# Low parts of split weights moved from GpSimd to VectorE, and a second set of weight load buffers

## The chip, the cores and the metric

The kernel runs on one core of one Trainium2 chip. The metric is the device time of one execution in microseconds. Engines are named as in the profile: PE is TensorE's matmul, PEld its weight load, DVE is VectorE, ACT is ScalarE, POOL is GpSimd, SP is SyncE, whose queue issues nearly all loads.

## The reference

Three blocks follow each other, all in float32:

```python
scores = scale * q @ k.T + bias            # 2 x 8 heads, 768 positions, 64 wide, local band + 8 global keys
x = softmax(scores) @ v                    # -> x: 1536 tokens x 512
xn = x / rms(x) * rms_g
x = (silu(xn @ w_gate) * (xn @ w_val)) @ w_out     # 512 -> 1536 -> 512, float64 weights
e = argmax(x @ r_gate)                     # 8 experts, one per token
out[e == i] = gate * (relu(x[e == i] @ w1[i]) @ w2[i])   # 512 -> 1024 -> 512
```

## The kernel before, in words

To keep float32 accuracy, each large product is made of three matmuls on float32r operands: every operand is split into a high part (its rounding to float32r) and a low part (the rest), and high x high, low x high and high x low are summed in PSUM. ACT makes the high part by a copy that rounds. The low part is a subtraction, value minus high part. Activations are split between ACT and DVE or POOL, weights between ACT and POOL, or ACT, DVE and POOL together.

The program has four parts, all written out in one stream for the usual inputs (`body(True)`):

- The attention, up to about 175 us, with the first part of the gated layer mixed into it.
- The gated layer in three sweeps over the 1536 features: sweep 0 takes blocks 0 to 2 of 128 features, sweep 1 blocks 3 to 6, sweep 2 blocks 7 to 11. Each sweep goes over six stages of 256 tokens (`moe_block`) and adds into the twelve row tiles `part0` to `part11` of 128 tokens. A stage and block needs 24 matmuls into two PSUM banks (L766), then tanh on ACT (L774), two products on DVE (`th` L775, `hf` L779), high part on ACT (L783), low part on POOL (L784), and then the output product (L803).
- The weights of this layer arrive as float64 and are turned into float32 while the sweep before runs: `convert64` takes a raw block of 512 KB, and for each half does one ACT operation (L333), four on DVE (L336, L339, L342, L345), the high part on ACT (L352) and the low part on POOL (L353). This is done 36 times. 9 belong to blocks 0 to 2 and are done during the attention; 27 to blocks 3 to 11 and are done behind it.
- The experts. In sweep 2 the tokens are routed (`route`), stored to the DRAM tensor `x1d` (L814), and their slots written to small tables. Expert by expert the token rows are gathered by POOL (L969), turned by PE (L982), multiplied by `w1` (L1055 for tiles of 128 tokens, L1029 for pairs of 256), and by `w2` (L1007), scaled on ACT (L1013) and scattered by POOL (L1014). Expert 0 has two tiles of 128 tokens, which take their own path (`expert_tile`: relu `hr` L1062, turned by PE L1069, split by L1073 and L1074); experts 1 to 7 go as pairs (`expert_pair`: high part `eh` L1037 on ACT, low part L1038 on DVE).

The weights of an expert come in eight chunks of 128 x 1024 (`prep_chunk`): SP loads a chunk into one of three raw buffers (L945, `NRAW = 3`), ACT makes the high part of all 1024 columns (L947), DVE the low part of the first 512 (L950, `NDV = 512`) and POOL that of the last 512 (L953). The raw buffer is free when all three are done. The finished chunk lies in a ring of 13 tiles (`ew`), where it stays until PE has used it.

```python
raw = rp.tile([P, DF2], F32, tag="raw", bufs=NRAW, name="rawe")
nc.sync.dma_start(out=..., in_=src)
cp = nc.scalar.activation(out=t[:, 0], in_=raw, func=ACTF.Copy)
nc.vector.tensor_tensor(out=t[:, 1, 0:NDV], in0=raw[:, 0:NDV], ..., op=ALU.subtract)
nc.gpsimd.tensor_tensor(out=t[:, 1, NDV:], in0=raw[:, NDV:], ..., op=ALU.subtract)
```

The order on each engine is set by the framework, which places the instructions by its own estimate of a timeline. Each engine then works through its list strictly in order, so an instruction that waits holds up all that stand behind it. The last loads before the experts, the copies of expert 1's first chunks (pinned behind `eh` of the first tile by `pin["act"]`) and the gathers are placed around the end of sweep 2.

Of the kernel before, what the change touches and what calls it, by code (L numbers as in the profile page):

```python
# [8 lines left out]
F32 = mybir.dt.float32  # L9
# [5 lines left out]
ALU = mybir.AluOpType  # L15
# [4 lines left out]
P = 128  # L20
B, H, S, D = 2, 8, 768, 64
NT, DM, DFF = B * S, H * D, 1536
NE, DF2 = 8, 1024
KD = DM // P
NP = H // 2
TT = NT // P
# [19 lines left out]
def kernel(  # L46
# [16 lines left out]
    nc = tc.nc  # L63
# [11 lines left out]
    NDV = 512  # L75
    HP = 0
    NRAW = 3
# [91 lines left out]
    def behind(i, first):  # L169

        tc.add_manual_dep(
            i.ins, first.ins.name,
            mybir.DependencyInfo(mybir.DependencyClass.NoSync, mybir.DependencyReason.DATA), reason="order",
        )
# [58 lines left out]

    part = [rp.tile([P, DM], F32, name=f"part{i}") for i in range(TT)]
    first_pairs = []
# [53 lines left out]
    def body(is_fast):  # L289
# [37 lines left out]
        def convert64(raw, hi, lo):  # L327
# [23 lines left out]
            else:  # L351
                nc.scalar.activation(out=hi, in_=tf, func=ACTF.Copy)  # L352
            nc.gpsimd.tensor_tensor(out=lo, in0=tf, in1=hi.bitcast(F32), op=ALU.subtract)  # L353

        weights = {}
        pin = {"act": None, "dve": None, "th": None}

# [576 lines left out]

        ring = {"n": 0, "pools": None, "xg": 0}

# [5 lines left out]

        def prep_chunk(src):
            raw = rp.tile([P, DF2], F32, tag="raw", bufs=NRAW, name="rawe")
            nc.sync.dma_start(out=raw if src.ndim == 2 else raw.rearrange("p (a d) -> p a d", a=2), in_=src)  # L945
            t = chunk_tile()
            cp = nc.scalar.activation(out=t[:, 0], in_=raw, func=ACTF.Copy)  # L947
            if pin["act"] is not None:
                behind(cp, pin["act"])
            nc.vector.tensor_tensor(  # L950
                out=t[:, 1, 0:NDV], in0=raw[:, 0:NDV], in1=t[:, 0, 0:NDV].bitcast(F32), op=ALU.subtract
            )
            nc.gpsimd.tensor_tensor(  # L953
                out=t[:, 1, NDV:], in0=raw[:, NDV:], in1=t[:, 0, NDV:].bitcast(F32), op=ALU.subtract
            )
            return t
# [225 lines left out]
        apool_cm.__exit__(None, None, None)  # L1182
        pin["act"] = None
        ea_cm = tc.tile_pool(name="ea", bufs=1, side="right")
# [56 lines left out]
        def prep_next(e, todo, n=1):  # L1241
            for _ in range(n):
                if todo:
                    d, f, c = todo.pop(0)
                    d[e].append(prep_chunk(f(e, c)))

# [117 lines left out]
```

## Time and profile before

| what | value |
|---|---|
| time, median of 3 runs | 671.49 us (669.6, 671.49, 671.59) |
| the profiled execution's own time | 670.62 us |
| its span, first to last instruction | 668.9 us |
| PE busy | 633.8 us, 95% |
| PEld busy | 564.5 us, 84% |
| DVE busy | 439.6 us, 66% |
| ACT busy | 318.3 us, 48% |
| POOL busy | 327.6 us, 49% |
| bytes moved | 83.00 MB, 124 GB/s over the span |

PE is busy for almost the whole span, so the time is that of PE's work plus the short stretches in which PE waits. Shares of the other engines are averages over parts with different loads; they are to be read by stretch. A row of waits says who waited, for which line, how long in total, how often and how long at most. A row of instruction groups gives the line, the engine, what it writes and reads, how often, its busy time and mean duration, and the idle time before it with its releaser.

### The profile page before, as it was taken

The numbers are of one execution on the slowest core, as the hardware profiler recorded it, in microseconds if no ns is written. First come the engines' busy times: TensorE is split into PE (matmuls) and PEld (weight loads), VectorE is DVE, ScalarE is ACT, GpSimd is POOL, SyncE is SP. The second block draws the span as 40 slices with busy tenths as digits, with TensorE's granted clock in tenths as the row PEclk, the third lists the DMA queues.
The fourth block names the chain that finished last, engine by engine and source line by source line (L and its number), as shares of the span: only waits on it lengthen the run. The fifth ranks groups of instructions, "written<-read, shape, count | busy, mean of one in ns | idle before, by whom it ended". The sixth has DMA issues, their size and how long they took to land. (4 is left out here: it accounts for less than half of the span.)

```text
span 668.9 us, 11962 instructions
## 1 busy us (share of the span) xinstructions
PE 633.8 (95%) x4280; PEld 564.5 (84%) x4281; DVE 439.6 (66%) x1203; ACT 318.3 (48%) x620; POOL 327.6 (49%) x358
## 2 busy tenths in 40 slices
PE   9998998999998999999999999899998999999992
PEld 4667888899997899999999999897787898899891
DVE  5765988974699887675369999944366554644410
ACT  3666798775555433334512221333455555564420
POOL 4425758572365544333222433462867758676400
PEclk9999999899999999999999999899999999999997
DMA  7536466541044432212321010321777677667200
GB/s 231 146 112 179 126 190 170 163 117 37 5 151 128 126 96 95 64 64 87 104 64 63 10 57 33 111 84 48 238 228 239 216 237 211 200 201 211 81 13 29
DMA packets 56570, 83.00 MB, mean 124 GB/s; under 512 B 7983, under 2 KB 38703, under 8 KB 56496
## 3 DMA queue, kind: packets, MB, share of 16 engines
q1 hardware_dynamic: 53552, 74.75, 36.8%
q0 software_dynamic: 2944, 7.35, 3.2%
q8 instruction: 37, 0.61, 0.4%
q14 instruction: 37, 0.30, 0.1%
HBM read 75.75 MB, written 7.39 MB: 124 GB/s over the span
## 5 line engine op out<-in xcount | busy, mean ns | idle before, releaser
L766 PE MATMUL pg<-xn,gv 128*128 128x256 f32 x1728 | 229.9, 286 | 2.8 <-DVE th L775 2.2
L766 PEld LDWEIGHTS pg<-xn,gv 128*128 128x128 f32 x1728 | 220.7, 193 | 10.4 <-DVE th L775 2.8
L953 POOL TENSOR_TENSOR ew<-rawe,ew 128x512 fp32r<-128x512 f32 x64 | 98.8, 1558 | 46.3 <-ACT ew L947 45.1
L803 PE MATMUL po<-ow,hid 128*128 128x512 f32 x432 | 113.6, 396 | 2.4 <-DVE th L775 1.1
L784 POOL TENSOR_TENSOR hid<-hf,hid 128x256 fp32r<-128x256 f32 x72 | 59.0, 823 | 108.5 <-ACT hid L783 108.1
L950 DVE TENSOR_TENSOR ew<-rawe,ew 128x512 fp32r<-128x512 f32 x64 | 67.1, 1054 | 63.7 <-ACT ew L947 61.0
L947 ACT ACTIVATE ew<-rawe 128x1024 fp32r<-128x1024 f32 x64 | 67.0, 1063 | 68.8 <-DMA rawe<-in_moe_w_dram 53.2
L1007 PE MATMUL py<-ew,eh 128*128 128x512 f32 x384 | 91.8, 396 | 2.6 <-DVE eh L1038 1.9
L803 PEld LDWEIGHTS po<-ow,hid 128*128 128x128 f32 x432 | 75.7, 189 | 15.3 <-DVE th L775 1.5
L1007 PEld LDWEIGHTS py<-ew,eh 128*128 128x128 f32 x384 | 71.3, 188 | 19.7 <-DVE eh L1038 2.6
L1029 PE MATMUL ph<-xs,ew 128*128 128x256 f32 x672 | 83.7, 284 | 0.4 <-DVE eh L1038 0.4
L1029 PEld LDWEIGHTS ph<-xs,ew 128*128 128x128 f32 x672 | 81.9, 191 | 1.4 <-DVE eh L1038 0.6
L783 ACT ACTIVATE hid<-hf 128x256 fp32r<-128x256 f32 x72 | 29.8, 415 | 87.3 <-DVE hf L779 87.1
L836 DVE CUSTOM_DVE_ANT_0 jk<-part,rgb 128x256 bf16<-128x256 f32 x128 | 59.5, 507 | 0.0
L558 ACT ACTIVATE pr<-pr,mx 128x256 f32<-128x256 f32 (+1 forms) x96 | 45.1, 484 | 15.0 <-DVE mx L554 14.1
L353 POOL TENSOR_TENSOR gv<-cv,gv 128x512 fp32r<-128x512 f32 x24 | 33.1, 1380 | 29.4 <-ACT gv L352 29.1
L775 DVE SCALAR_TENSOR_TENSOR th<-th,pg 128x256 f32<-128x256 f32 x72 | 29.8, 414 | 26.8 <-ACT th L774 26.6
L774 ACT ACTIVATE th<-pg 128x256 f32<-128x256 f32 x72 | 26.9, 376 | 33.3 <-PE pg L766 31.8
L342 DVE SCALAR_TENSOR_TENSOR cv<-raw,cv 128x512 uint32<-128x512 uint32 x36 | 38.0, 1054 | 0.8
L779 DVE SCALAR_TENSOR_TENSOR hf<-th,pg 128x256 f32<-128x256 f32 x72 | 29.7, 414 | 9.3 <-PE pg L766 7.0
L812 DVE TENSOR_TENSOR part<-part,po 128x512 f32<-128x512 f32 x36 | 23.3, 682 | 19.0 <-PE po L803 19.0
L569 PE MATMUL pp<-ident,pr 128*128 128x128 f32 x176 | 32.5, 281 | 2.9 <-ACT ptS L577 2.3
(175 smaller groups left out, 882.1 us busy)
## 6 DMA issues: line engine op xcount, KB each, us to landing
rawe<-in_moe_w_dram SPq DMA_DIRECT2D x64, 512.0 KB, 3.8
raw<-in_moe_w_gate_dram SPq DMA_DIRECT2D x12, 512.0 KB, 3.7
raw<-in_moe_w_val_dram SPq DMA_DIRECT2D x12, 512.0 KB, 3.6
raw<-in_moe_w_out_dram SPq DMA_DIRECT2D x12, 512.0 KB, 3.5
kn<-in_k_dram SPq DMA_DIRECT2D x28, 192.0 KB, 3.3
qn<-in_q_dram SPq DMA_DIRECT2D x36, 128.0 KB, 3.2
vn<-in_v_dram SPq DMA_DIRECT2D x16, 192.0 KB, 3.3
x1d<-part SPq DMA_DIRECT2D x12, 256.0 KB, 2.5
```

What stands on the lines that cost most here:

```text
L342: nc.vector.scalar_tensor_tensor(out=t, in0=hw, scalar=0xC0000000, in1=t, op0=ALU.bitwise_and, op1=ALU.bitwise_or)
L353: nc.gpsimd.tensor_tensor(out=lo, in0=tf, in1=hi.bitcast(F32), op=ALU.subtract)
L558: pin["act"] = nc.scalar.activation(out=pr[:, j, 0:n], in_=pr[:, j, 0:n], func=ACTF.Exp, bias=mx[:, t, j:j + 1], scale=-1.0,)
L766: nc.tensor.matmul(out=pg[:, 0:n_], lhsT=gv[:, i, a, kk, :], rhs=x[st][:, kk, :], start=(n == 0), stop=(n == 3 * KD - 1),)
L784: nc.gpsimd.tensor_tensor(out=hh[:, 1], in0=hf, in1=hh[:, 0].bitcast(F32), op=ALU.subtract)
L803: nc.tensor.matmul(out=po, lhsT=hid[mi][:, a, t * P:(t + 1) * P], rhs=ow[:, c, :], start=(mi == 0 and n == 0), stop=(mi == len(ms) - 1 and ...
L836: nc.vector.tensor_tensor_reduce(out=jk, in0=part[i0 + t][:, h * 256:(h + 1) * 256], in1=rgb[h][:, e, :], scale=1.0, scalar=0.0, op0=ALU.m ...
L947: cp = nc.scalar.activation(out=t[:, 0], in_=raw, func=ACTF.Copy)
L950: nc.vector.tensor_tensor(out=t[:, 1, 0:NDV], in0=raw[:, 0:NDV], in1=t[:, 0, 0:NDV].bitcast(F32), op=ALU.subtract)
L953: nc.gpsimd.tensor_tensor(out=t[:, 1, NDV:], in0=raw[:, NDV:], in1=t[:, 0, NDV:].bitcast(F32), op=ALU.subtract)
L1007: last_mm["py"] = nc.tensor.matmul(out=py, lhsT=hid(m, a, j), rhs=w2t[m // 2][:, c, (m % 2) * DM:(m % 2 + 1) * DM], start=(n == 0), stop=( ...
L1029: nc.tensor.matmul(out=ph[:, 0:CAP], lhsT=w1t[kk][:, a, m * P:(m + 1) * P], rhs=x[:, kk, :], start=(n == 0), stop=(n == 3 * KD - 1),)
```

## The change

Three things are changed. First, from the end of the attention on (`pin["sweep"]`), the low parts of the gated layer's weights are made by DVE instead of POOL: 27 subtractions of 128 x 512. Second, the chunks of experts 1 to 7 (`spare=1`) get their whole low part, 1024 columns, from DVE, and POOL has no part in them: 56 subtractions of 512 columns leave POOL, and 56 on DVE become twice as wide. Third, the row tiles `part` become halves of six larger tiles `duo`, and `duo3` to `duo5` (rows 6 to 11, free once their stage is routed and stored) serve as three more raw buffers, in turn with the three old ones. The eight chunks of expert 0 keep the old split and the old buffers.

```diff
-    part = [rp.tile([P, DM], F32, name=f"part{i}") for i in range(TT)]
+    duo = [rp.tile([P, 2, DM], F32, name=f"duo{i}") for i in range(TT // 2)]
+    part = [duo[i // 2][:, i % 2] for i in range(TT)]
...
-            nc.gpsimd.tensor_tensor(out=lo, in0=tf, in1=hi.bitcast(F32), op=ALU.subtract)
+            (nc.vector if pin["sweep"] else nc.gpsimd).tensor_tensor(
+                out=lo, in0=tf, in1=hi.bitcast(F32), op=ALU.subtract
+            )
...
-        def prep_chunk(src):
-            raw = rp.tile([P, DF2], F32, tag="raw", bufs=NRAW, name="rawe")
+        def raw_tile(spare):
+            ring["r"] += spare
+            if spare and ring["r"] % 2:
+                return duo[TT // 4 + ring["r"] // 2 % (TT // 4)].rearrange("p a d -> p (a d)")
+            return rp.tile([P, DF2], F32, tag="raw", bufs=NRAW, name="rawe")
+
+        def prep_chunk(src, spare=0):
+            raw = raw_tile(spare)
...
+            nd = DF2 if spare else NDV
             nc.vector.tensor_tensor(
-                out=t[:, 1, 0:NDV], in0=raw[:, 0:NDV], in1=t[:, 0, 0:NDV].bitcast(F32), op=ALU.subtract
-            )
-            nc.gpsimd.tensor_tensor(
-                out=t[:, 1, NDV:], in0=raw[:, NDV:], in1=t[:, 0, NDV:].bitcast(F32), op=ALU.subtract
-            )
+                out=t[:, 1, 0:nd], in0=raw[:, 0:nd], in1=t[:, 0, 0:nd].bitcast(F32), op=ALU.subtract
+            )
+            if nd < DF2:
+                nc.gpsimd.tensor_tensor(
+                    out=t[:, 1, nd:], in0=raw[:, nd:], in1=t[:, 0, nd:].bitcast(F32), op=ALU.subtract
+                )
...
-        pin["act"] = None
+        pin["act"], pin["sweep"] = None, True
...
-                    d[e].append(prep_chunk(f(e, c)))
+                    d[e].append(prep_chunk(f(e, c), int(e > 0)))
```

Since the framework orders anew, instructions also change places. The attention, the last sweep and its routing keep their order on all engines except SP's loads. Line numbers of the changed kernel are 1 to 11 higher: L336, L339, L342, L345 become L337, L340, L343, L346; L775 and L779 become L778 and L782; L945 becomes L954, L947 becomes L956, L1062 becomes L1073.

On DVE, in sweep 0 behind the attention, two conversions of block 5 (`cv` is the scratch tile of a conversion, `gv5` its result, `th` and `hf` belong to the sweep) stand like this before:

```order
L336 TENSOR_SCALAR cv_2542<-cv_2542 128x512
L339 TENSOR_SCALAR cv_2542<-cv_2542 128x512
L775 SCALAR_TENSOR_TENSOR th_2830<-th_2830,pg_2804 128x256
L342 SCALAR_TENSOR_TENSOR cv_2542<-raw_2540,cv_2542 128x512
L779 SCALAR_TENSOR_TENSOR hf_2833<-th_2830,pg_2817 128x256
L345 SCALAR_TENSOR_TENSOR cv_2542<-raw_2540,cv_2542 128x512
L336 TENSOR_SCALAR cv_2565<-cv_2565 128x512
L775 SCALAR_TENSOR_TENSOR th_2864<-th_2864,pg_2838 128x256
L339 TENSOR_SCALAR cv_2565<-cv_2565 128x512
L779 SCALAR_TENSOR_TENSOR hf_2867<-th_2864,pg_2851 128x256
L342 SCALAR_TENSOR_TENSOR cv_2565<-raw_2563,cv_2565 128x512
L345 SCALAR_TENSOR_TENSOR cv_2565<-raw_2563,cv_2565 128x512
```

In the changed kernel the same two conversions stand like this:

```order
L337 TENSOR_SCALAR cv_2536<-cv_2536 128x512
L340 TENSOR_SCALAR cv_2536<-cv_2536 128x512
L337 TENSOR_SCALAR cv_2559<-cv_2559 128x512
L343 SCALAR_TENSOR_TENSOR cv_2536<-raw_2534,cv_2536 128x512
L340 TENSOR_SCALAR cv_2559<-cv_2559 128x512
L778 SCALAR_TENSOR_TENSOR th_2858<-th_2858,pg_2832 128x256
L346 SCALAR_TENSOR_TENSOR cv_2536<-raw_2534,cv_2536 128x512
L343 SCALAR_TENSOR_TENSOR cv_2559<-raw_2557,cv_2559 128x512
L782 SCALAR_TENSOR_TENSOR hf_2861<-th_2858,pg_2845 128x256
L346 SCALAR_TENSOR_TENSOR cv_2559<-raw_2557,cv_2559 128x512
L354 TENSOR_TENSOR gv5_2533<-cv_2536,gv5_2533 128x512
L354 TENSOR_TENSOR gv5_2533<-cv_2559,gv5_2533 128x512
```

The conversions now go in pairs, and the two subtractions (L354) stand at the end of a pair; the first needs ACT's high part of `cv_2536`, which ACT can make while DVE does three more operations. In sweep 1 the conversions go singly, and of its 15 subtractions five stand directly behind the L346 that they depend on, four have one `th` or `hf` product between, and two have two others of the next conversion beside one.

On ACT, behind the first tile of expert 0 up to `hr` of its second tile, before (`ew` is a finished chunk, `rawe` a raw buffer, `yo` an output, `xs` the turned rows):

```order
L1073 ACTIVATE eh_6045<-trh_6040 128x512
L947 ACTIVATE ew_6151<-rawe_6149 128x1024
L947 ACTIVATE ew_6157<-rawe_6155 128x1024
L947 ACTIVATE ew_6163<-rawe_6161 128x1024
L1013 ACTIVATE yo_6073<-py_6048,wt0_5124 128x512
L985 ACTIVATE xs_6111<-trs_6112 128x4x128
L985 ACTIVATE xs_6119<-trs_6120 128x4x128
L985 ACTIVATE xs_6119<-trs_6127 128x4x128
L947 ACTIVATE ew_6189<-rawe_6187 128x1024
L1062 ACTIVATE hr_6134<-ph_6135 128x512
L947 ACTIVATE ew_6195<-rawe_6193 128x1024
L947 ACTIVATE ew_6201<-rawe_6199 128x1024
```

The row after these is `hr`'s second half (L1062). In the changed kernel:

```order
L956 ACTIVATE ew_6144<-duo3_116 128x1024
L956 ACTIVATE ew_6149<-rawe_6147 128x1024
L956 ACTIVATE ew_6153<-duo4_117 128x1024
L956 ACTIVATE ew_6178<-rawe_6176 128x1024
L1024 ACTIVATE yo_6067<-py_6042,wt0_5118 128x512
L996 ACTIVATE xs_6105<-trs_6106 128x4x128
L996 ACTIVATE xs_6113<-trs_6114 128x4x128
L996 ACTIVATE xs_6113<-trs_6121 128x4x128
L1073 ACTIVATE hr_6128<-ph_6129 128x512
L956 ACTIVATE ew_6182<-duo5_118 128x1024
L956 ACTIVATE ew_6187<-rawe_6185 128x1024
L956 ACTIVATE ew_6282<-rawe_6280 128x1024
```

Four copies instead of three stand ahead of the turned rows, none between them and the first `hr`, and four (the three last rows and one more, of `duo3`) between the two halves of `hr`. On SP, from the last stores of stage 4 on, the changed kernel has:

```order
L954 DMA duo4_117<-in_moe2_w1_dram 128x1024
L954 DMA rawe_6147<-in_moe2_w1_dram 128x1024
L954 DMA rawe_6176<-in_moe2_w1_dram 128x1024
L954 DMA rawe_6185<-in_moe2_w2_dram 128x2x512
L817 DMA x1d_101<-duo5_118 128x512 x2
L954 DMA duo5_118<-in_moe2_w2_dram 128x2x512
L1241 DMA mt1_6089<-meta_d0_102 128x30
L1241 DMA mt1_6089<-meta_d1_103 128x30
L1107 TENSOR_LOAD need_7875
L1107 ISA x2
L954 DMA duo3_116<-in_moe2_w2_dram 128x2x512
L954 DMA rawe_6240<-in_moe2_w2_dram 128x2x512
```

Before, this place held three loads of `rawe`, the two stores, the two `mt` loads (slots of the gathers) and then the next load of `rawe`. Now the loads into `duo4` and `duo5` are added to it, and the one into `duo3` stands a little ahead.

## Rows read from the trace of the kernel before

**Rows 1.** Windows of all engines: busy us (x instructions), granted clock, DMA share, GB/s
```profile
175.00:225.00 50.00, 47.02 (x327) 42.80 (x327) 44.37 (x71) 27.95 (x58) 27.87 (x23) 1.00 0.38 117
225.00:330.00 105.00, 104.01 (x752) 97.63 (x752) 69.78 (x129) 42.33 (x81) 39.68 (x39) 1.00 0.28 91
...
480.00:530.00 50.00, 45.35 (x298) 40.66 (x297) 31.07 (x39) 28.98 (x45) 35.55 (x27) 1.00 0.73 236
530.00:656.00 126.00, 126.00 (x794) 113.45 (x793) 55.58 (x85) 59.09 (x95) 72.03 (x50) 1.00 0.53 165
```

**Rows 2.** What PE waited for from 175 to 225 us, total, times, longest
```profile
PE po L803 <- DVE th L775: 1.1, 1, 1.1
PE pg L766 <- DVE th L775: 1.0, 2, 0.7
```

**Rows 3.** What PE waited for from 455 to 530 us
```profile
PE trh L1069 <- ACT hr L1062: 2.3, 2, 2.1
PE py L1007 <- DVE eh L1038: 1.9, 1, 1.9
```

**Rows 4.** Groups of instructions from 175 to 225 us, of the conversions
```profile
L342 DVE SCALAR_TENSOR_TENSOR cv<-raw,cv 128x512 uint32<-128x512 uint32 x12 | 16.8, 1398 | 0.2
...
L353 POOL TENSOR_TENSOR gv<-cv,gv 128x512 fp32r<-128x512 f32 x9 | 12.2, 1357 | 10.1 <-ACT gv L352 10.1
...
L352 ACT ACTIVATE gv<-cv 128x512 fp32r<-128x512 f32 x9 | 5.6, 629 | 6.0 <-DVE cv L345 6.0
```

**Rows 5.** Line L342, all its instructions: ns min/median/max
```profile
L342 DVE SCALAR_TENSOR_TENSOR cv<-raw,cv x36: 677/694/1758, 15.1 to 308.6; 128x512 uint32<-128x512 uint32 x36
```

**Rows 6.** Timeline in sweep 0: start us, us, engine, line, operation, idle before
```profile
202.59 1.29 POOL L353 TENSOR_TENSOR gv<-cv,gv 128x512 fp32r<-128x512 f32 x1 [1.29 <-ACT gv L352]
202.67 1.75 DVE L342 SCALAR_TENSOR_TENSOR cv<-raw,cv 128x512 uint32<-128x512 uint32 x1
...
205.54 4.92 PE L766 MATMUL pg<-xn,gv 128*128 128x256 f32 x36 [0.73 <-DVE th L775]
```

**Rows 7.** Line L784 of POOL, all its instructions
```profile
L784 POOL TENSOR_TENSOR hid<-hf,hid x72: 723/744/1197, 72.7 to 449.7; 128x256 fp32r<-128x256 f32 x72
```

**Rows 8.** Timeline between sweep 2 and the experts, 450 to 480 us
```profile
454.58 1.02 SPq L814 DMA_DIRECT2D x1d<-part  x2
...
462.99 1.63 SPq L1230 DMA_DIRECT2D mt<-meta_d  x2
...
466.38 2.95 ACT L947 ACTIVATE ew<-rawe 128x1024 fp32r<-128x1024 f32 x3
...
474.27 3.81 POOL L953 TENSOR_TENSOR ew<-rawe,ew 128x512 fp32r<-128x512 f32 x3
...
475.60 2.88 SPq L945 DMA_DIRECT2D rawe<-in_moe_w_dram  x3
```

**Rows 9.** Timeline of ACT from 475 to 487 us
```profile
479.56 1.06 ACT L947 ACTIVATE ew<-rawe 128x1024 fp32r<-128x1024 f32 x1 [3.09 <-DMA rawe<-in_moe_w_dram]
...
484.31 1.06 ACT L947 ACTIVATE ew<-rawe 128x1024 fp32r<-128x1024 f32 x1 [1.49 <-DMA rawe<-in_moe_w_dram]
485.27 0.58 ACT L1062 ACTIVATE hr<-ph 128x512 f32<-128x512 f32 x1
```

**Rows 10.** Timeline in expert 1
```profile
506.29 3.76 POOL L953 TENSOR_TENSOR ew<-rawe,ew 128x512 fp32r<-128x512 f32 x3
506.31 4.30 DVE L950 TENSOR_TENSOR ew<-rawe,ew 128x512 fp32r<-128x512 f32 x1 [0.91 <-ACT ew L947]
...
511.00 2.34 PE L1007 MATMUL py<-ew,eh 128*128 128x512 f32 x9 [1.93 <-DVE eh L1038]
```

**Rows 11.** Groups of instructions from 455 to 656 us
```profile
L950 DVE TENSOR_TENSOR ew<-rawe,ew 128x512 fp32r<-128x512 f32 x56 | 60.5, 1087 | 62.1 <-ACT ew L947 59.4 <-PE ph L1029 2.0
...
L1038 DVE SCALAR_TENSOR_TENSOR eh<-ph,eh 128x256 fp32r<-128x256 f32 x56 | 21.5, 418 | 19.8 <-ACT eh L1037 19.8
```

**Rows 12.** DMA issues: KB each, median us to landing
```profile
rawe<-in_moe_w_dram SPq DMA_DIRECT2D x64, 512.0 KB, 3.8
```

More of the change, by code (lines that the diff above doesn't have):

```diff
@@ L352, in convert64 @@
                 nc.scalar.activation(out=hi, in_=tf, func=ACTF.Copy)
-            nc.gpsimd.tensor_tensor(out=lo, in0=tf, in1=hi.bitcast(F32), op=ALU.subtract)
+            (nc.vector if pin["sweep"] else nc.gpsimd).tensor_tensor(
+                out=lo, in0=tf, in1=hi.bitcast(F32), op=ALU.subtract
+            )
         weights = {}
-        pin = {"act": None, "dve": None, "th": None}
+        pin = {"act": None, "dve": None, "th": None, "sweep": False}
         def prep_steps(ms, pool, nslot):
@@ L932, in route @@
                 )
-        ring = {"n": 0, "pools": None, "xg": 0}
+        ring = {"n": 0, "pools": None, "xg": 0, "r": 0}
         def chunk_tile():
```

## The prediction, made before the changed kernel ran

> **What bounds the kernel now.** I read the windows by stretch first. PE is what fills the time: from 530 to 656 us it is busy for all of 126 us, from 225 to 330 for 104.01 of 105 [rows 1]. Only two stretches that the change touches lose more: 175 to 225 us (47.02 of 50, so 2.98 lost) and 480 to 530 us (45.35 of 50, so 4.65 lost) [rows 1]. Engines that are idle beside a busy PE cost nothing, so all that this change can win lies in these few microseconds, unless PE's own work changes, and it does not: the same matmuls are done.
>
> The table of PE's waits names what is late. In the first stretch it is DVE's `th` product, for 1.1 and 1.0 us [rows 2]; in the second ACT's `hr` (2.3 us, the longest 2.1) and DVE's `eh` (1.9 us, once) [rows 3]. So the question is what stood ahead of these three on their own engines.
>
> For `th` and `eh` it is a subtraction that took far longer than its work. In sweep 0 DVE's L342 began at 202.67 while POOL's L353 had just begun at 202.59; POOL ended at 203.88, and DVE at 204.42, after 1.75 us, though half of all L342 take 0.694 or less [rows 5, 6]. DVE thus did its work almost wholly after POOL had finished, and PE sat idle for 0.73 us for the `th` behind it [rows 6]. In expert 1 three POOL subtractions in a row held one L950 of DVE for 4.30 us, and PE waited 1.93 us for the `eh` behind that [rows 10], though L950 is as wide as L342 and also reads two tiles from SBUF. Such an operation of DVE stands still while POOL does the same.
>
> For `hr` it is a load. ACT's copy L947 began at 484.31, after 1.49 us of waiting for its raw buffer to land, and `hr` came only behind it, at 485.27 [rows 9]. The loads were late because all three raw buffers were held: ACT had made their high parts from 466.38 on, but POOL came to its halves only at 474.27, and SP could issue the next load at 475.60 [rows 8].
>
> **The change part by part.**
>
> *Sweep 0, 12 conversions.* L342 averages 1.398 us there against an undisturbed 0.694 [rows 4, 5], so without POOL's L353 it gives back up to 12 x 0.704 = 8.4 us of DVE. The 12 subtractions that DVE takes over cost 12 x 0.694 = 8.3 us, taking L342 as the nearest row of 512 columns from two SBUF tiles. DVE's load of 44.37 us [rows 1] therefore stays about what it is, 44.3. What changes is its form: single blocks of 1.4 to 1.75 us go, and POOL keeps only the `hid` subtractions of 0.744 us [rows 7], which can still hold DVE. I take back half of PE's loss, 1.5 us, with bounds of 0 (the `hid` subtractions hit as often as L353 did) and 3.0 (all of it).
>
> The moved instruction also waits: L354 needs ACT's high part, which takes 0.629 us [rows 4], and behind it on DVE stand `th` and `hf`, for which PE waits. In sweep 0 the order pairs the conversions, so that three other operations fill this time; I cost it at nothing there. In sweep 1 five of 15 stand directly behind their L346. They wait some 0.7 us each, and four more some 0.3, together 4.7 us. With 15 x 0.694 = 10.4 us of work DVE comes to about 85 of 105 us there. I take 0.4 us of this as reaching PE, since PE lost only 0.99 us in 105 with DVE at 69.78 [rows 1]; the bounds are 0 and 4.7, every wait passed on.
>
> *The end of sweep 2 and expert 0.* Six chunks instead of three are now loaded before the copies begin. The load into `duo5` stands ahead of the slot tables on SP. It may go when the stores issued at 454.58 and behind have landed; a load takes 3.8 us [rows 12], and the tables were issued at 462.99 [rows 8], so it is over before them: nothing. The copies are four instead of three and start at 466.4 as before. DVE's subtraction is now 1024 wide. No row has this; it lies between 0.694 (as if width cost nothing) and 1.39 (twice the 512 columns of L342 [rows 5]). From 256 columns (0.418 us, L1038 [rows 11]) to 512 it grows by 0.276, so 512 more cost 0.55, and I take 1.24. The first buffer is free at about 466.4 + 1.06 + 1.24 = 468.7, against 475.60: the loads start again 7 us sooner.
>
> The copy that now stands last but one ahead of the second half of `hr` reads the fourth of these loads (`rawe_6280`). With 3.8 us for the first and some 2.4 for each further one (the copies at 479.56 and 484.31 each waited for a load, and there is one between them, so two loads took 4.75 us [rows 9]) it lands at 468.7 + 3.8 + 3 x 2.4 = 479.7. That is 4.6 us before 484.31, and one copy more (1.06 us) stands behind it, so `hr` comes at about 485.27 - 4.6 + 1.06 = 481.7 instead of 485.27, over 1 us before PE wants it (485.27 + 0.58 - 2.1 = 483.8). Of the 2.1 us I take 1.8 as gained. If five gathers of 256 KB delay these loads by all their bytes, 1.3 MB at 236 GB/s [rows 1] or 5.6 us, the wait is not gone but grows by about 2.5; that is the other bound.
>
> *Experts 1 to 7.* With no POOL subtraction left, the 1.9 us for `eh` [rows 3] should go whole: the longest thing ahead of `eh` is now one subtraction of 1.24 us. The bounds are 0 and 1.9. DVE's subtractions average 1.087 us now [rows 11], so 56 of them cost 56 x 0.15 = 8.6 us more; DVE sits idle for 62.1 us just before them [rows 11] and PE waits for nothing from 530 us on, so this is free. The tail behind the last matmul is untouched.
>
> *Sum.* 1.5 - 0.4 + 1.8 + 1.9 = 4.8 us. The profiled execution took 670.62 us by itself (span 668.9), 0.87 below the median of 671.49. 670.62 - 4.8 = 665.8, and I give 666.0 for the median of the changed kernel.
>
> A rule speaks against this. The Trainium skill, in "Perfetto Trace Analysis", section "Optimizing Scalar/DVE Operations", says that moving operations between GpSimd and VectorE may not help, because both read SBUF through one shared port. By it the terms 1.5 and 1.9 would be 0 and the sum 1.4. The trace bears out its ground, the 4.30 us of one L950 [rows 10], but not its conclusion: DVE already pays POOL's time on top of its own.
>
> **The rivals.** *Everything that is lost comes back*: 2.98 in sweep 0, 0.99 in sweep 1, 2.1 and 1.9 in the experts, 8.0 us in all, or 662.6. For it: each wait has a cause that the change removes. Against it: `hid` stays on POOL and DVE's load stays. Chance 0.14.
>
> *The waits only change sides*: in sweep 0 the load of DVE is as before, so nothing comes back; sweep 1 loses 1.0; the fourth load comes late enough for `hr` to keep its wait; only the 1.9 remain. 670.62 - 0.9 = 669.7, no change that can be told. For it: the unchanged 44.3 us of DVE and the four copies between the halves of `hr`. Against it: the longest blocks on DVE are gone. The same result comes if the new buffers are not used as early as the order says. Chance 0.17.
>
> *Slower: DVE inherits POOL's waits for ACT.* POOL sat idle 10.1 us for nine subtractions, 1.12 each, until ACT had made the high part [rows 4]. POOL could afford that; on DVE `th` and `hf` stand behind. If ACT's list, in which the high part stands among copies that wait for DVE and PE, makes DVE wait as long, 12 x 1.12 = 13.5 us come to 44.3, 57.8 in a stretch of 50, and the stretch grows by 7.8: 670.62 + 7.8 - 3.7 = 674.7. It begins to bind from 5.7 / 12 = 0.47 us of waiting per subtraction and outweighs the 3.7 of the experts from 0.78 on. For it: five subtractions of sweep 1 without cover. Against it: the pairs in sweep 0. Chance 0.13.
>
> **How the numbers follow.** The forecast has 0.56. A measurement of this kernel can tell about 0.3%, 2 us, from no change. Forecast and full return are faster (0.70), changed sides is the same (0.17), inherited waits is slower (0.13). The range of 662 to 672 holds the forecast with its bounds, full return and changed sides, and leaves out the last.
>
> **What would show it.** Right: L343 at about 0.7 to 0.9 us on average, chunk subtractions at 1.24 with none above 1.5, the loads behind the slot tables issued near 469, no wait of PE for `eh` over 1 us, `hr` before 484. Wrong: PE waits for `th` totalling more than 2.1 us before 225, DVE idle in front of L354 for more than 0.5 us each, or a copy between the halves of `hr` that waits for a load past 482.

## The result and the profile after

The changed kernel took **662.79 us** (median of four runs, 661.66 to 665.5) against 671.54 for the kernel before on the same chip; the ratio is 0.9874, 95% interval 0.984 to 0.9908. So it is faster by 8.75 us, 1.3%. The profiled execution took 662.19 us (span 660.4), 8.43 less than the one of before (670.62). TensorE's granted clock averages 0.985 in both, so the difference is not the clock's. L342, L353, L950 and L1038 of before are L343, L354, L960 and L1049 now; POOL's half of a chunk is L964 where it remains.

The windows of the profile after, in the form of [rows 1] (busy us with instructions in brackets for PE, PEld, DVE, ACT, POOL, then granted clock, DMA share, GB/s):

```profile
175.00:225.00 50.00, 50.00 (x360) 47.05 (x359) 47.00 (x92) 29.84 (x61) 11.85 (x12) 1.00 0.39 117
225.00:330.00 105.00, 104.28 (x758) 98.18 (x758) 74.38 (x140) 42.95 (x82) 21.52 (x26) 1.00 0.29 91
480.00:530.00 50.00, 49.22 (x304) 43.91 (x305) 31.14 (x41) 28.76 (x45) 8.11 (x8) 1.00 0.70 231
```

From 175 to 225 us PE is busy throughout and does 360 matmuls where it did 327 [rows 1]. From 480 to 530 us it loses 0.78 us in place of 4.65. POOL has about half its work or less in each. PE waits for nothing in the first of these stretches any more; from 455 to 530 us this is left, against [rows 3]:

```profile
PE trh L1080 <- ACT hr L1073: 0.9, 2, 0.7
PE py L1018 <- ACT eh L1084: 0.8, 1, 0.8
PE trs L993 <- DMA duo<-x1d,tk: 0.3, 1, 0.3
```

The wait of 1.9 us for `eh` of L1049 is gone, `hr` has 0.9 us of 2.3, and two other small waits are there. The groups of DVE from 175 to 225 us, against [rows 4]:

```profile
L343 DVE SCALAR_TENSOR_TENSOR cv<-raw,cv 128x512 uint32<-128x512 uint32 x13 | 9.5, 728 | 0.0
...
L354 DVE TENSOR_TENSOR gv<-cv,gv 128x512 fp32r<-128x512 f32 x9 | 7.0, 791 | 1.8 <-ACT gv L353 1.7
...
L354 DVE TENSOR_TENSOR ow<-cv,ow 128x512 fp32r<-128x512 f32 x4 | 3.7, 933 | 0.0
```

L343 went from 1398 ns to 728. The subtractions, new on DVE, take 791 and 933 ns on average, and DVE stands idle for 1.8 us in all before the nine of `gv` and for nothing before the four of `ow`. Some still last longer, where POOL's `hid` subtraction runs beside them.

The chunk subtractions of experts 1 to 7, all of them (ns min/median/max), and three of SP's loads behind the slot tables, from the timeline (start us, us):

```profile
L960 DVE TENSOR_TENSOR ew<-duo,ew x28: 1218/1224/1227, 463.0 to 616.5; 128x1024 fp32r<-128x1024 f32 x28
L960 DVE TENSOR_TENSOR ew<-rawe,ew x28: 1215/1224/1228, 464.1 to 617.9; 128x1024 fp32r<-128x1024 f32 x28
```

```profile
464.26 0.39 SPq L954 DMA_DIRECT2D duo<-in_moe_w_dram  x1
465.40 0.38 SPq L954 DMA_DIRECT2D rawe<-in_moe_w_dram  x1
...
476.55 0.33 SPq L954 DMA_DIRECT2D duo<-in_moe_w_dram  x1
```

No subtraction is longer than 1.228 us; half the width had taken 4.30 us [rows 10] and 4.965 at most. The loads resume at 464.26. Everything stands 6 us earlier here (the slot tables are issued at 456.97, before at 462.99), so that is 7.3 us behind the tables, where it had been 12.6 [rows 8].

**Where the time came from**, by the timeline: the start of the same matmul in both executions, and for the last one its end. `pg` counts the matmuls of the sweeps' first products, `py` those of the experts' second.

| matmul | before, us | after, us | difference |
|---|---|---|---|
| 200th `pg` (attention ending) | 166.57 | 167.77 | +1.20 |
| 600th `pg` | 244.27 | 240.61 | -3.66 |
| 1008th `pg` | 315.84 | 311.45 | -4.39 |
| 24th `py` | 471.89 | 466.90 | -4.98 |
| last `py` of expert 1 | 515.02 | 507.43 | -7.59 |
| last `py` of expert 2 | 539.35 | 530.88 | -8.48 |
| end of the last matmul | 656.14 | 647.66 | -8.48 |

The first stretch gives 4.9 us, the next 0.7, the way from there to the 24th `py` (in expert 0) 0.6, and that to the end of expert 2 3.5. Nothing is gained or lost in the last five experts.

### The profile page after: what moved, and what is told of

Same layout as the page of the kernel before. It is cut to its first block, busy times and chain, and to the rows that moved or that the text cites. A ratio compares the mean times of both kernels' runs of the same rounds, so it can differ in the third digit from the quotient of the medians.

```text
span 660.4 us, 11819 instructions
## 1 busy us (share of the span) xinstructions
PE 631.6 (96%) x4280; PEld 563.5 (85%) x4281; DVE 452.6 (69%) x1230; ACT 319.5 (48%) x620; POOL 204.3 (31%) x275
## 5 line engine op out<-in xcount | busy, mean ns | idle before, releaser
L769 PE MATMUL pg<-xn,gv 128*128 128x256 f32 x1728 | 227.4, 284 | 2.3 <-DVE th L778 1.5
L806 PEld LDWEIGHTS po<-ow,hid 128*128 128x128 f32 x432 | 75.4, 188 | 12.6 <-ACT hid L786 0.9
L1025 POOL DMA_INDIRECT out_dram<-yo,tk x16 | 16.5, 1031 | 141.3 <-ACT yo L1024 109.9
L839 DVE CUSTOM_DVE_ANT_0 jk<-duo,rgb 128x256 bf16<-128x256 f32 x128 | 59.5, 508 | 0.0
L960 DVE TENSOR_TENSOR ew<-rawe,ew 128x1024 fp32r<-128x1024 f32 (+1 forms) x36 | 40.8, 1133 | 14.7 <-ACT ew L956 14.6
L1049 DVE SCALAR_TENSOR_TENSOR eh<-ph,eh 128x256 fp32r<-128x256 f32 x56 | 23.2, 423 | 37.5 <-ACT eh L1048 37.3
L960 DVE TENSOR_TENSOR ew<-duo,ew 128x1024 fp32r<-128x1024 f32 x28 | 34.1, 1223 | 20.3 <-ACT ew L956 19.6
L956 ACT ACTIVATE ew<-rawe 128x1024 fp32r<-128x1024 f32 x36 | 38.1, 1058 | 13.6 <-PE pg L769 5.8
L778 DVE SCALAR_TENSOR_TENSOR th<-th,pg 128x256 f32<-128x256 f32 x72 | 29.8, 414 | 16.3 <-ACT th L777 16.0
L1048 ACT ACTIVATE eh<-ph 128x256 fp32r<-128x256 f32 x56 | 21.1, 383 | 38.5 <-PE ph L1040 38.5
L956 ACT ACTIVATE ew<-duo 128x1024 fp32r<-128x1024 f32 x28 | 29.4, 1058 | 19.4 <-PE py L1018 19.4
L782 DVE SCALAR_TENSOR_TENSOR hf<-th,pg 128x256 f32<-128x256 f32 x72 | 29.8, 416 | 9.3 <-PE pg L769 8.0
```

Of the source, the lines that this page charges most:

```text
L769: nc.tensor.matmul(out=pg[:, 0:n_], lhsT=gv[:, i, a, kk, :], rhs=x[st][:, kk, :], start=(n == 0), stop=(n == 3 * KD - 1),)
L778: nc.vector.scalar_tensor_tensor(out=th, in0=th, scalar=1.0, in1=pss[0][:, 0:n_], op0=ALU.add, op1=ALU.mult)
L782: nc.vector.scalar_tensor_tensor(out=hf, in0=th, scalar=0.5, in1=pss[1][:, 0:n_], op0=ALU.mult, op1=ALU.mult)
L806: nc.tensor.matmul(out=po, lhsT=hid[mi][:, a, t * P:(t + 1) * P], rhs=ow[:, c, :], start=(mi == 0 and n == 0), stop=(mi == len(ms) - 1 and ...
L839: nc.vector.tensor_tensor_reduce(out=jk, in0=part[i0 + t][:, h * 256:(h + 1) * 256], in1=rgb[h][:, e, :], scale=1.0, scalar=0.0, op0=ALU.m ...
L960: nc.vector.tensor_tensor(out=t[:, 1, 0:nd], in0=raw[:, 0:nd], in1=t[:, 0, 0:nd].bitcast(F32), op=ALU.subtract)
```

## The experiments

All are cut from the changed kernel. "Gated" stands for the 27 conversions behind the attention, "chunks" for the weights of experts 1 to 7. V is VectorE alone, G is as before (GpSimd, or half of each chunk). The kernel before took 671.82, 671.71 and 671.88 us on the three chips used. The ratio is not exactly the quotient of two medians; differences in us given below as "about" are worked out from it.

| kernel | gated | chunks | raw buffers | us | ratio to before, 95% interval |
|---|---|---|---|---|---|
| e1_gated_only | V | G | 3 | 666.13 | 0.9922 (0.9897 to 0.9947) |
| e2_chunks_only | G | V | 3 | 667.38 | 0.9934 (0.9913 to 0.9955) |
| e3_buffers_only | G | G | 6 | 677.31 | 1.0098 (1.0065 to 1.0132) |
| e4_chunks_buffers | G | V | 6 | 667.99 | 0.9952 (0.9928 to 0.9976) |
| x1_no_spare | V | V | 3 | 660.82 | 0.9855 (0.982 to 0.989) |
| after_again | V | V | 6 | 662.55 | 0.988 (0.9844 to 0.9915) |
| c0_duo_only | G | G | 3 | 670.87 | 0.9993 (0.9972 to 1.0014) |
| m1_both_engines | V, and G again | G | 3 | 680.07 | 1.0125 (1.0097 to 1.0153) |
| m2_double_dve | V twice | V | 6 | 664.16 | 0.9898 (0.9861 to 0.9934) |
| m3_pool_memset | V, and G fills | G | 3 | 679.52 | 1.0106 (1.0085 to 1.0126) |
| x2_all_dve | V, all 36 | V, expert 0 too | 3 | 655.89 | 0.9763 (0.9742 to 0.9784) |
| x3_hid_dve | V, and `hid` | V | 3 | 660.48 | 0.9846 (0.9815 to 0.9878) |

**One part at a time.** First, the gated weights alone.

```diff
-            raw = raw_tile(spare)
+            raw = raw_tile(0)
-            nd = DF2 if spare else NDV
+            nd = NDV
```

> Only the 27 low parts of the gated layer's weights go to VectorE; chunks and buffers of the experts as before. Theory (GpSimd's reads held VectorE up, and PE behind it): PE's waits and short gaps between 175 and 225 us go as in the full change, 4 to 5 us less, 666.5 to 667.5; the waits for hr and eh near 485 and 510 stay as before. Rival (the gain is in the experts' buffers, sweep 0 only looks better because DVE's order fell differently): within 1 us of before.

Measured: 0.9922. Its window from 175 to 225 us and its PE waits from 455 to 530 us:

```profile
175.00:225.00 50.00, 50.00 (x360) 47.11 (x360) 46.93 (x92) 30.16 (x61) 11.37 (x11) 1.00 0.39 118
```

```profile
PE ph L1040 <- DVE eh L1049: 2.4, 1, 2.4
PE trh L1080 <- ACT hr L1073: 1.8, 2, 1.6
```

The first stretch is that of the changed kernel, and the waits in the experts are still there. So this part is worth 0.8%, about 5.2 us, by itself. The starts of the matmuls agree closely: from the 200th to the 600th `pg` it is 72.84 us in this kernel, the changed one, x1_no_spare and after_again, and 77.69 to 77.78 in the kernel before, e2_chunks_only, e3_buffers_only, e4_chunks_buffers and c0_duo_only, which leave the gated part to POOL.

Second, the chunks alone, with three raw buffers.

```diff
-        pin["act"], pin["sweep"] = None, True
+        pin["act"], pin["sweep"] = None, False
-            raw = raw_tile(spare)
+            raw = raw_tile(0)
```

> Only the chunks of experts 1 to 7 go to VectorE alone, with the three old buffers. Theory: the wait for eh (1.9 us) goes and buffers come free about 6 us sooner, so about half of the wait for hr goes: 2 to 3 us less, 668.5 to 669.5. Rival (the loads bound this place and need six buffers): the wait for hr stays at 2 us, 669.5 to 670.

Measured: 0.9934, about 4.4 us. From 175 to 225 us PE waits for `th` as before, 1.1 and 1.0 us [rows 2]; from 455 to 530 us:

```profile
PE trs L993 <- DMA duo<-x1d,tk: 2.8, 1, 2.8
PE py L1018 <- DVE eh L1085: 0.5, 1, 0.5
...
PE trh L1080 <- ACT hr L1073: 0.2, 1, 0.2
```

`hr` waits 0.2 us without any extra buffer. Half of that wait was expected to stay: a miss. But PE now stands 2.8 us for a gather of rows (`trs` turns them) on the way to the same tile, and by that the copies ahead of `hr` have more time: the wait has in part changed its place. Why the gather is late was not tried apart. The chunk loads resume 5.7 us behind the slot tables here and run beside the gathers, and single gathers took POOL up to 1.95 us to issue (in the kernel before 1.36 at most). In the changed kernel the gathers issued from 460 to 480 us took 3.3/6.6/8.8 us to land (min/median/max), in the kernel before, from 460 to 485 us, 3.2/3.8/5.9.

The two parts multiply to 0.9922 x 0.9934 = 0.9857, against 0.9874 and 0.988 for the whole change and 0.9855 for both without the buffers. Within these intervals they are independent of each other.

Third, the six buffers alone.

```diff
-        pin["act"], pin["sweep"] = None, True
+        pin["act"], pin["sweep"] = None, False
-            nd = DF2 if spare else NDV
+            nd = NDV
```

> Only the six raw buffers; POOL keeps its half of every chunk. Theory: POOL's subtractions still begin only behind its gathers and still hold DVE; the wait for hr shrinks by some 1 us, the wait for eh stays near 2 us: 0 to 1.5 us less, 670 to 671.5. Rival (loads bound this place): the waits for hr and eh both go, 3.5 to 4 us less, 667.5.

Measured: 1.0098, **slower** by about 6.6 us: a miss by both accounts. Its PE waits from 440 to 660 us, and its timeline where two of them arise:

```profile
PE py L1018 <- DVE eh L1049: 4.0, 1, 4.0
PE py L1018 <- DVE eh L1085: 3.1, 2, 2.7
PE py L1018 <- ACT eh L1084: 2.5, 1, 2.5
```

```profile
484.91 1.28 POOL L964 TENSOR_TENSOR ew<-duo,ew 128x512 fp32r<-128x512 f32 x1
485.77 5.90 DVE L960 TENSOR_TENSOR ew<-rawe,ew 128x512 fp32r<-128x512 f32 x1 [2.40 <-ACT ew L956]
486.13 1.29 POOL L964 TENSOR_TENSOR ew<-rawe,ew 128x512 fp32r<-128x512 f32 x1
487.38 1.28 POOL L964 TENSOR_TENSOR ew<-duo,ew 128x512 fp32r<-128x512 f32 x1
488.63 2.50 POOL L964 TENSOR_TENSOR ew<-rawe,ew 128x512 fp32r<-128x512 f32 x2
491.60 1.27 DVE L1085 TENSOR_TENSOR eh<-trh,eh 128x512 fp32r<-128x512 f32 x2
...
554.00 7.51 DVE L960 TENSOR_TENSOR ew<-rawe,ew 128x512 fp32r<-128x512 f32 x1 [0.21 <-ACT ew L956]
```

With more buffers ACT runs ahead, POOL's half-chunks queue up behind each other, and five of them in a row hold one subtraction of DVE for 5.90 us; it ends 0.54 us after the last of them. `eh` of L1085 stands behind it. (The wait for ACT's `eh`, 2.5 us, is another: ACT stood 2.03 us for a load ahead of it.) The longest, from 554.00, lasted 7.509 us, where the kernel before had 4.965 at most; behind it came PE's longest wait, 4.0 us for `eh` of L1049, and then a granted clock of 0.55 from 562.8 to 566.6 us. By the starts of the matmuls this is where the time went: expert 3, in which it lies, takes 5.6 us more than in the kernel before, and the way from the 24th `py` to the end of expert 1 only 0.7 more. More buffers made the lock worse as long as GpSimd had work to queue.

Fourth, chunks and buffers together, without the gated part.

```diff
-        pin["act"], pin["sweep"] = None, True
+        pin["act"], pin["sweep"] = None, False
```

> Chunks by VectorE alone with six buffers, the gated layer as before. Theory: the two parts are independent, so this gains what the full change gains less e1: 3.5 to 4.5 us, 667 to 668, with PE's waits before 225 us as before. Rival (gain of the experts' buffers alone): all 8.7 us, 663.

Measured: 0.9952, not to be told from the 0.9934 without the buffers. Then both moves without the buffers.

```diff
-            raw = raw_tile(spare)
+            raw = raw_tile(0)
```

> The changed kernel with three raw buffers in place of six; both moves to VectorE stay. Theory (the two moves do everything, the six buffers nothing, since the kernel with the chunks moved and three buffers had already lost the waits for hr and for eh): 661 to 664 us, within 0.3% of the changed kernel, and no wait for hr above 1 us. Rival (the moves need the loads 8 us earlier, as the prediction had it): a wait of 2 us for hr or for a gather behind sweep 1, 665 to 667 us.

Measured: 660.82 us, 0.9855; the changed kernel itself, run once more, 662.55, 0.988.

> The changed kernel once more, beside the next three on the same chip. Theory and rival alike: 660 to 664 us, a ratio of 0.984 to 0.990 to the kernel before. If it lies within 0.3% of the kernel with the same moves and three raw buffers (0.9855), the six buffers do nothing.

As the theory said: the buffers do nothing for the time here. The profile of x1_no_spare has no wait for `hr` above 0.2 us; one of 2.4 us, for the gathered and transposed rows (`xs`), is there, as the rival had it (ACT stood 2.23 us for a load ahead of them), but the time is not above the changed kernel's.

**The joined tiles.** In the profiles of the changed kernel and of the four experiments up to e4_chunks_buffers the 200th `pg` stood 0.9 to 1.6 us later than before. This kernel has only the pairs.

```diff
-        pin["act"], pin["sweep"] = None, True
+        pin["act"], pin["sweep"] = None, False
-            raw = raw_tile(spare)
+            raw = raw_tile(0)
-            nd = DF2 if spare else NDV
+            nd = NDV
```

> The kernel before with nothing but the row tiles joined in pairs (part[i] as halves of duo); no instruction moves to another engine, three raw buffers. Theory: the later start of the sweep (the 200th matmul of pg 0.9 to 1.2 us later in each kernel that has the pairs) comes from the joined tiles, in the attention: 672 to 673 us, the attention's last transpose about 1 us later than before, all waits behind it as before. Rival: the joined tiles change nothing, the shift is scatter between profiles: within 0.1% of the kernel before and no later milestone.

Measured: 0.9993, and its 200th `pg` stands at 164.64, 1.93 us *earlier*. The theory fell: over the profiles of kernels that leave the attention alone the 200th `pg` lies from 2.0 us earlier (m2_double_dve) to 1.8 later (x3_hid_dve) than before, so the +1.20 of the table above is no more than executions scatter. What scatters is TensorE's granted clock from 60 to 130 us: 1.00 in c0_duo_only and m2_double_dve (200th `pg` at 164.64 and 164.58), 0.98 in x1_no_spare (165.62), 0.95 in the kernel before, the changed one and the others (166.57 to 168.35). m3_pool_memset and x2_all_dve, which change the attention, are left out of this.

**Lock or latency?** The gated part could have gained because POOL's own 1.36 us were in the way of the matmul, or because DVE stood still beside it. Here DVE makes the low part and POOL makes it again, for nobody.

```diff
+            if pin["sweep"]:
+                idle = rp.tile([P, n], F32, tag="idle", bufs=1, name="idle")
+                nc.gpsimd.tensor_tensor(out=idle, in0=tf, in1=hi.bitcast(F32), op=ALU.subtract)
```

(and the edit of e1_gated_only.)

> The kernel with the gated weights' low parts by VectorE alone (chunks halved as before, three raw buffers), and GpSimd computes each of the 27 low parts a second time into a tile that nobody reads. So GpSimd is as busy as before, but nothing waits for its result except the buffer cv. Theory (the loss before was VectorE standing still while GpSimd's subtraction reads SBUF): the gain goes: the waits for th before 225 us come back, L354's idle or its duration grows, 670 to 674 us. Rival (the loss was GpSimd's own duration on the way to the matmul, 1.36 us in place of 0.69): as without the second subtraction, 665 to 667.5 us.

Measured: 680.07 us, 8.4 above the kernel *before* and 13.9 above e1_gated_only; the stretch from the 200th to the 600th `pg` takes 86.07 us in place of 72.84. The largest of its PE waits and its DVE groups from 175 to 225 us, and a piece of its timeline (L359 is the second subtraction):

```profile
PE pg L772 <- DVE th L781: 2.4, 3, 1.9
```

```profile
L343 DVE SCALAR_TENSOR_TENSOR cv<-raw,cv 128x512 uint32<-128x512 uint32 x10 | 12.6, 1263 | 0.0
L354 DVE TENSOR_TENSOR gv<-cv,gv 128x512 fp32r<-128x512 f32 x8 | 11.5, 1444 | 0.9 <-ACT gv L353 0.9
```

```profile
203.65 1.34 POOL L359 TENSOR_TENSOR idle<-cv,gv 128x512 f32<-128x512 f32 x1 [2.08 <-ACT gv L353]
...
204.09 1.44 DVE L354 TENSOR_TENSOR gv<-cv,gv 128x512 fp32r<-128x512 f32 x1
...
208.21 1.71 POOL L359 TENSOR_TENSOR idle<-cv,gv 128x512 f32<-128x512 f32 x1 [2.08 <-ACT gv L353]
208.72 1.75 DVE L343 SCALAR_TENSOR_TENSOR cv<-raw,cv 128x512 uint32<-128x512 uint32 x1
```

L354 ends at 205.53, 0.54 us after POOL's subtraction (204.99); the L343 of 1.75 us ends 0.55 us after the one at 208.21. Nobody reads what POOL makes, and yet PE's waits are back, larger than before. The rival falls: POOL's own time is not on the way to the matmul here. The rows show the lock at work, and it explains the waits for `th`. The expected 670 to 674 was too low; the likely reason is that DVE now has both its own subtraction and the lock, where the kernel before had only the lock. One limit: POOL's reading also holds the buffer `cv` longer. From 175 to 330 us ACT stood 8.4 us for it before its next conversion (in the kernel before 7.3). DVE waited only 0.2 us for these conversions, but what stands behind them on ACT comes late as well: from 225 to 330 us PE's largest wait is for ACT's part of `hid`, 3.4 us. How much of the loss came this way was not separated.

**How much room has DVE?** In the changed kernel DVE is busy for 47.00 of the 50 us. This kernel does each gated subtraction twice.

```diff
-            (nc.vector if pin["sweep"] else nc.gpsimd).tensor_tensor(
-                out=lo, in0=tf, in1=hi.bitcast(F32), op=ALU.subtract
-            )
+            for _ in range(1 + pin["sweep"]):
+                (nc.vector if pin["sweep"] else nc.gpsimd).tensor_tensor(
+                    out=lo, in0=tf, in1=hi.bitcast(F32), op=ALU.subtract
+                )
```

> The changed kernel with each of the 27 gated subtractions done twice by VectorE (the same values written again). Theory (in 175 to 225 us VectorE is busy 47 of 50 us, so 12 more of 0.69 us find 3 us of room; in sweep 1 it has 20 us of room in 125): TensorE waits for th again before 225 us and the time is 3 to 6 us above the changed kernel, 666 to 669 us. Rival (VectorE's share there includes time that gives way, no wait appears): 662 to 664 us.

Measured: 0.9898, overlapping the changed kernel's intervals, so the theory is not borne out. Its window:

```profile
175.00:225.00 50.00, 50.00 (x362) 47.14 (x362) 49.28 (x97) 27.48 (x57) 13.24 (x12) 1.00 0.34 106
```

DVE is busy for 49.28 of 50 us and PE for all 50; no wait for `th` is left, and one for a gather behind the sweeps (2.5 us) is longer than in the changed kernel. Eleven L343 lie in the stretch in place of 13: the conversions, which run ahead of the matmuls, slip into the next stretch. That is nearly free but not quite: from the 200th to the 600th `pg` it is 73.00 us (changed kernel 72.84), from there to the 1008th 72.12 (70.84), 1.4 us more in all. The intervals can't show that, and in the profiled execution a quicker attention covers it (200th `pg` at 164.58). A busy share near one is no bound while the queue is ahead of what is waited for.

**Fills in place of reads.** The question was whether any work of POOL holds DVE, or only one that reads two tiles.

```diff
+            if pin["sweep"]:
+                idle = rp.tile([P, n], F32, tag="idle", bufs=1, name="idle")
+                for _ in range(3):
+                    nc.gpsimd.memset(idle, 0.0)
```

(and the edit of e1_gated_only.)

> The kernel with the gated low parts by VectorE alone (chunks halved, three raw buffers), and GpSimd, in place of the second subtraction that cost 14 us, fills an unread tile three times with zeros: it writes SBUF and reads nothing. Theory (what holds VectorE is GpSimd's reading of two operands): the gain stays, 665 to 668 us, L354 near 0.75 us on average. Rival (any work of GpSimd in SBUF holds VectorE, or GpSimd's longer queue makes the low parts of hid late): L354 above 1.0 us or waits for hid, 670 us or more.

Measured: 679.52 us, far from the 665 to 668 expected, but it answers another question. Its row of the fills (ns min/median/max, first and last start):

```profile
L360 POOL MEMSET idle<- x81: 514/524/814, 12.6 to 126.3; 128x512 f32 x81
```

A fill waits for nobody, so all 81 were done by 126.3 us, in the attention, where POOL has work of its own, and none in the sweeps. Whether a POOL operation that only writes holds DVE stays open.

**Further along the same way.** Two versions with three raw buffers. The first moves every low part of a weight, those of the attention's nine blocks and of expert 0 too:

```diff
-        pin = {"act": None, "dve": None, "th": None, "sweep": False}
+        pin = {"act": None, "dve": None, "th": None, "sweep": True}
-            raw = raw_tile(spare)
+            raw = raw_tile(0)
-            nd = DF2 if spare else NDV
+            nd = DF2
```

> Three raw buffers, and VectorE alone computes the low parts of every weight: of expert 0's chunks too (8 GpSimd subtractions of 1.48 us go), and of the 9 blocks converted in the attention (9 of 1.38 us). Theory (TensorE has no wait left that ends at one of these subtractions): within 0.3% of the changed kernel, 660 to 664 us. Rival (GpSimd's last subtractions still hold VectorE on the way to the rank sums behind sweep 1 and in the attention): 1 to 3 us less, 658 to 661 us.

Measured: **655.89 us** (655.13 to 657.16), 0.9763, the fastest, and its interval lies clear of every other. It gained more than either account had: 6.7 us against the changed kernel run beside it. PE's waits of the changed kernel from 380 to 480 us, and of this one:

```profile
PE rk L895 <- DVE oh L888: 2.0, 3, 1.4
PE trs L993 <- DMA duo<-x1d,tk: 0.3, 1, 0.3
PE trh L1080 <- ACT hr L1073: 0.2, 1, 0.2
```

```profile
PE trs L993 <- DMA duo<-x1d,tk: 1.3, 1, 1.3
PE py L1018 <- DVE eh L1085: 0.4, 1, 0.4
PE rk L895 <- DVE oh L888: 0.3, 1, 0.3
PE trh L1080 <- ACT hr L1073: 0.2, 1, 0.2
```

The rank sums wait 1.7 us less, and a gather costs 1.0 more. These waits make up a small part of the 6.7 us. By the starts of the matmuls, against the changed kernel run beside it (after_again), 1.6 us come before the 600th `pg`, 3.5 between the 1008th `pg` and the 24th `py` (151.91 us here, 155.42 there), and 0.3 behind. The 1.6 come although the granted clock from 60 to 130 us is lower here (0.93, there 0.95), so they probably go with the attention's blocks. Beside the 3.5 the granted clock from 380 to 480 us is 1.00 here and 0.98 there; x3_hid_dve, which left expert 0's chunks halved, has the same clock, the same short wait for the rank sums and 152.05 us, so this part isn't the move of these chunks alone. Which of the two additions gives what was not tried apart: open.

The second moves POOL's `hid` subtractions instead:

```diff
-                nc.gpsimd.tensor_tensor(out=hh[:, 1], in0=hf, in1=hh[:, 0].bitcast(F32), op=ALU.subtract)
+                nc.vector.tensor_tensor(out=hh[:, 1], in0=hf, in1=hh[:, 0].bitcast(F32), op=ALU.subtract)
```

(with the edit of x1_no_spare.)

> Both moves, three raw buffers, and VectorE takes GpSimd's last steady work of the sweeps as well: the 72 low parts of hid (128x256, 0.83 us on GpSimd, about 0.41 us on VectorE by its other 128x256 operations). Theory (VectorE works ahead of TensorE: 12 more subtractions in 50 us showed no wait, and 72 more of 0.41 us are 29 us over 290 us): no gain and no loss above 0.3%, 659 to 663 us, and L354 and L343 lose their long ones of 1.2 us. Rival (VectorE now stands in its queue behind ScalarE's copy of each hid, 72 times 0.3 to 0.6 us): TensorE waits for th or hid again, 664 to 672 us.

Measured: 660.48 us, 0.9846: no difference to x1_no_spare that can be told, as the theory said. The two profiled executions differ, though: from the 1008th `pg` to the 24th `py` it is 152.05 us here and 155.55 there, while the 200th `pg` stands 2.7 us later, with a granted clock of 0.95 in place of 0.98 from 60 to 130 us. Whether the move is worth the 3.5 us stays open. Its DVE groups from 175 to 225 us:

```profile
L343 DVE SCALAR_TENSOR_TENSOR cv<-raw,cv 128x512 uint32<-128x512 uint32 x12 | 8.2, 687 | 0.0
...
L354 DVE TENSOR_TENSOR gv<-cv,gv 128x512 fp32r<-128x512 f32 x9 | 6.1, 686 | 1.3 <-ACT gv L353 1.3
```

With POOL silent in this stretch (0.66 us of work) both average the undisturbed 0.69 us. So what was left above that in the changed kernel, 728 and 791 ns, was `hid`; it cost PE nothing in this stretch, in which PE is busy throughout with it and without it.

## Why the prediction was right, and where it was not

The forecast was faster, 666.0 us, a sum of 4.8; the profiled executions differ by 8.43. The measured 662.79 lies close to the lower end of the range of 662 to 672: the direction and the reasons held, and one term was far too small.

*Sweep 0, 1.5 us.* **This is the step that failed, in size:** "I take back half of PE's loss, 1.5 us", with bounds of 0 and of "3.0 (all of it)". It gave 4.9 us by the starts of the 200th and 600th `pg`, and the gated part alone gives 5.2. Both the half and the upper bound were wrong. The half: `hid` does hit L343 and L354, but for PE nothing follows there. The bound: 2.98 us was PE's idle time in the window, and PE's loss is larger than its idle time. Counted in matmuls the stretch went from 327 to 360; at 50.00 / 360 = 0.139 us each, 33 more are 4.6 us. This could have been read from [rows 1]: the next stretch, nearly always busy, has 752 matmuls in 105 us, or 358 in 50. That records of a matmul that waits also look longer would explain the difference; it was not tried apart. The reason itself (DVE pays POOL's time on top of its own) was right, as m1_both_engines shows from the other side, within the limit named there.

*Sweep 1, -0.4 us.* It gave 0.7 us instead (600th to 1008th `pg`: 71.57 us before, 70.84 after). DVE's waits for ACT came about as foreseen: 3.7 us of idle time before the 14 L354 from 225 to 330 us, against 4.7 for the 15 named. None of it reached PE: the conversions run ahead, and even twice the subtractions cost only 1.3 us there (m2_double_dve).

*`hr`, 1.8 us, and `eh`, 1.9 us.* Together 3.7 us; PE's loss from 480 to 530 us fell by 3.9, and the starts from the 24th `py` on give 3.5. `eh` went whole and stayed away. For `hr` the reason was half wrong: the loads do resume earlier, but six buffers are not needed for it; e2_chunks_only has three, and they resume 5.7 us behind the slot tables. The step's own arithmetic had it right without knowing: "The first buffer is free at about 466.4 + 1.06 + 1.24" uses no fourth buffer, only a subtraction that no longer stands in POOL's queue. The feared collision with the gathers exists, and it shows on both sides. ACT's copy of the fourth load came at 477.46, after 1.25 us of waiting for it: 20.5 us behind the slot tables, where the forecast's 479.7 is 16.7 behind them, and this is what `hr` still waits for. And PE waits for a gather, 2.8 us in e2_chunks_only, 0.3 in the changed kernel. So the term came out near its size, but in part by waits that changed their place.

*The chunk subtraction, 1.24 us estimated:* 1.224. *The load into `duo5` and the tail, nothing:* the slot tables came 6.0 us earlier and not later, and from the last matmul to the end it is 12.8 us in both. Two sums of the prediction are off without harm to the result: by its own figures `hr`'s wait could have grown by 5.6 - 4.6 + 1.06 = 2.1 us, not 2.5; and all its lower bounds together give -7.2 us or 677.8, which the range of 662 to 672 does not hold.

*The rivals.* Full return (662.6) comes closest in time but not in composition: more than was counted came back in the sweeps, and about 2 us of waits remain or are new in the experts. "The waits only change sides" fell with the terms 1.5 and 1.9 being 4.9 and 1.9. The Trainium skill, "Perfetto Trace Analysis", section "Optimizing Scalar/DVE Operations", concludes from the shared port that moving operations between GpSimd and VectorE might not help; here it helped, by 1.3%. "DVE inherits POOL's waits for ACT" needed 0.47 us of waiting per subtraction; it was 0.14 (1.8 us before 13).

## What to carry to other kernels

Where VectorE and GpSimd both subtract tiles of SBUF, add GpSimd's duration to VectorE's when you ask what is late: here the operations that VectorE does in half the time could move there for nothing. Bound what a stretch can give back by the number of matmuls that it holds, compared with a stretch of the same work that is busy throughout, and not by TensorE's idle time alone. When a wait goes, look whether it has come back one step earlier. Before you add buffers, look whose queue gets longer by it.

## What the runs showed of the hardware

An operation of VectorE on 512 columns with two inputs from SBUF that meets a subtraction of GpSimd ends 0.54 to 0.56 us after it, in the kernel before [rows 6, 10], in m1_both_engines and in e3_buffers_only alike. One with a single input is held too: L336 of the kernel before took 0.414 us at least and 1.290 at most, and that longest one ended 0.28 us after a subtraction of GpSimd (L353). And such an operation does not get in between: while GpSimd's subtractions followed each other, a VectorE operation of 0.69 us stood through five of them (5.90 us, at most 7.509). The Trainium skill, "SBUF — State Buffer", section "Who interferes with whom", has it that an operation of VectorE with two SBUF inputs contends with a GpSimd instruction that reads SBUF; these rows agree. That whole rows of GpSimd instructions pass ahead of the waiting one is what I had not expected, and it stands ahead of the largest loss of the kernel with six buffers alone (the 7.509 us, then PE's 4.0).
